# An earlier release for one weights load, and one conversion a step earlier, in a fused attention and feed-forward kernel

## The chip, the cores and the metric

The kernel runs on one core of a Trainium2 chip. The metric is the device time of one execution in microseconds (us). The kernel before takes 544.36 us (median of 3 runs, 543.9 to 545.09).

The core's engines work side by side, each in the order in which its instructions stand. TensorE (PE in the profile, its weight loads PEld) multiplies matrices, VectorE (DVE) and ScalarE (ACT) work elementwise, GpSimd (POOL) makes masks and constants here, and SyncE (SP) issues most of the transfers (DMAs). Engines wait for each other through semaphores.

## The reference, cut to what matters

A linear attention (4 batches, 8 heads, 768 positions, head size 48) feeds a feed-forward block (3072 tokens, width 384, inner width 2048).

```python
for t in range(S):
    cur = einsum('bhd,bhe->bhde', u[None] * kt, vt)
    y[:, :, t] = einsum('bhd,bhde->bhe', rt, state + cur)
    state = wt[:, :, :, None] * state + einsum('bhd,bhe->bhde', kt, vt)

x = y.transpose(0, 2, 1, 3).reshape(B * S, H * D)
h = x @ w_in
out = (h - tanh(h)) @ w_out
```

## The kernel before

**Tiling.** The 3072 tokens are eight blocks of 384 (four batches, two halves of the sequence each). Attention goes by chunks of 64 tokens. For a block it is made of scores inside a chunk ("own", the diagonal, and "earlier", the part off the diagonal), updates (each chunk's keys times values, from which the states follow) and results (scores times values plus states times receptances). The eight heads lie in four pairs, and the pairs in two halves, `HALVES`: `h1` is handled first, then `h2`.

**Feed-forward.** A block's feed-forward has 16 steps `f`. A step multiplies the block's `x` with one tile of `w_in` (three matmuls of 128x384; the profile counts two for each, so six, L871), copies the product out on ScalarE (`h`, L876), forms the activation on VectorE and ScalarE (the square L902, ScalarE's square `qa` L905, two products L879), and a few steps later multiplies with a tile of `w_out` (L950 in block 0). While one block's feed-forward runs, the next block's attention is made in its steps, by a written plan: `plan(i)` says which piece belongs to which step.

**Weights.** The weights arrive as 64-bit raw words in 16 units of 768 KB (`load_weights`, L251). A unit alternates between `w_in` and `w_out`, in the order of `UNITS`, and holds the tiles of two steps. `convert` turns a unit into float32 pairs with three operations on ScalarE (L264: one into `w_sb`, two into a scratch tile `up`) and then one merge on VectorE (L268, in place in `w_sb`). A matmul with a tile of that unit waits for the merge. Five raw buffers rotate.

**Boot.** Before block 0's feed-forward can start, `boot` makes block 0's attention with nothing to hide it behind. Its order is written out by hand: every engine's instructions stand in the order of the calls. PE's order in the first part is: small matmuls that only keep PE busy (L312, L305), own scores of h1 (L494), a transposition (L517), earlier scores of h1 (L494 again), updates of h1 (L616), a transposition, then results of h1 (L697, L679), then the same for h2.

SP issues in the boot: the inputs of block 0, raw unit 0, raw unit 1 (the "second raw weights"), then some small pieces of `xT` and further units. `begin_behind(ins, then)` adds a wait: `then` does not begin before `ins` is done. For raw unit 1 the instruction waited for is `blk.done`, the last matmul of whatever `gram` or `update_half` last set it.

**Conversions in block 0.** From unit 2 on, conversions are spread over block 0's steps. `PIECES[f]` says how many of ScalarE's conversion operations step `f` takes. In `converting` they come from one list, three per unit; the merge goes with the third. All but one of a step's operations stand ahead of `qa`, the last behind it. The merges of a step (`made_up`) are run by VectorE in the next step (`extra`), ahead of that step's square. A step's loads (`loads` in `plan`) wait for the step's copy of its product on ScalarE.

The unit whose merge step 8 needs is the eighth, `(0, 4)`: its third operation stands in step 6 before the change.

Of the kernel before, what the change touches and what calls it, by code (L numbers as in the profile page):

```python
# [72 lines left out]
RAWS = 5  # L73
LAG = 2
LAST = 5
PIECES = 0, 0, 2, 3, 3, 2, 4, 4, 3, 3, 3, 4, 4
UNITS = [(0, 0), (0, 1)] + [u for j in range(NF // 2 - 2) for u in ((1, j), (0, j + 2))] + [(1, NF // 2 - 2),
                                                                                      (1, NF // 2 - 1)]
LATE = 3
# [47 lines left out]
def kernel(  # L127
# [12 lines left out]
    nc = tc.nc  # L140
# [107 lines left out]
    def load_weights(n, queue):  # L248
        raw = conv.tile([P, 2 * DM, 2], I32, name="raw", tag="raw")
        src = weights[UNITS[n]].bitcast(I32).rearrange("p (n two) -> p n two", two=2)  # L250
        return *UNITS[n], raw, queue.dma_start(out=raw, in_=src)  # L251

    def convert(part, j, raw, _, tiles=1):

        lo, hi = raw[:, :, 0], raw[:, :, 1]
        a = w_sb[:, part, 2 * j:2 * j + 2].rearrange("p f c -> p (f c)").bitcast(I32)
        up = conv.tile([P, 2 * DM], I32, name="up", tag="up", bufs=4)
        low, high = (up.bitcast(t).rearrange("p (n two) -> p n two", two=2)[:, :, i]  # L260
                     for i, t in enumerate((U16, F16)))

        def scaled(to, of, scale, bias=0.0):
            return lambda: nc.scalar.activation(out=to, in_=of, func=AF.Copy, scale=scale, bias=bias)  # L264

        return [scaled(a.bitcast(F32), hi.bitcast(F32), HIGH_SCALE), scaled(high, hi.bitcast(F32), SIGN_SCALE),
                scaled(low, lo.bitcast(U32), *LOW)], [
                lambda of=slice(i * 2 * DM // tiles, (i + 1) * 2 * DM // tiles): nc.vector.scalar_tensor_tensor(  # L268
                    out=a[:, of], in0=a[:, of], scalar=3, in1=up[:, of], op0=ALU.logical_shift_left,
                    op1=ALU.bitwise_or) for i in range(tiles)]  # L270
# [43 lines left out]
    def begin_behind(ins, then):  # L314
        tc.add_manual_dep(then.ins, ins.ins.name, mybir.DependencyInfo(
            mybir.DependencyClass.Sync, mybir.DependencyReason.DATA))
# [3 lines left out]
    class Block:  # L320
# [186 lines left out]
        def own(self, ps, p0, **fill):  # L507
            return self.masked(ps, "k", "r", masks["diagonal"], p0, **fill)

        def earlier(self, ps, p0, **fill):  # L510
            return self.masked(ps, "post", "pre", masks["above"], p0, **fill)
# [370 lines left out]
    def slight(h, n, i, f):  # L882

        s, qa = (dense.tile([P, NB], F32, name=name, tag=name) for name in ("s", "qa"))
        q, j = divmod(f, 2)
        if i in fast:
            g = G[:, g_at(q, "0" + "ab"[j]):g_at(q, "2" + "ab"[j]) + 1].rearrange("p t c -> p (t c)")
        else:  # L890
            g = ring(sums, 0, n)
        if n in light:
            at = 2 * blocks_n + light.index(n)
            nc.scalar.activation(out=s, in_=h, func=AF.Square)  # L894
            nc.scalar.activation(out=qa, in_=s, func=AF.Square, bias=shift[:, 4:5])  # L895
            junk = work.tile([P, UP * NCH * LP], BF16, name="junk", tag="junk", bufs=1)
            nc.scalar.activation(out=junk[:, 0:NB], in_=s, func=AF.Relu, bias=shift[:, 5:6],  # L897
                                 accum_out=excess[:, at:at + 1])
            square = first = []
        else:  # L900
            at = plain.index(n)
            square = [lambda: nc.vector.tensor_tensor_reduce(  # L902
                out=s, in0=h, in1=h, scale=1.0, scalar=0.0, op0=ALU.mult, op1=ALU.max,
                accum_out=top[:, at:at + 1])]
            first = [lambda: nc.scalar.activation(out=qa, in_=s, func=AF.Square, bias=shift[:, 4:5])]  # L905
        return g, first, square, [product(h, h, TOP, s, ALU.mult), product(g, qa, REST, h, ALU.add)]
# [198 lines left out]
    def more_weights(queue):  # L1105
        raws.append(load_weights(more_weights.n, queue))
        more_weights.n += 1
        return raws[-1][-1]
# [3 lines left out]
    def run(ops):  # L1112
        for op in ops:
            op()

    def converting(pieces, n):

        made = []
        for _ in range(n):
            if not pieces:  # L1120
                on_act, on_dve = convert(*raws.pop(0))
                pieces += zip(on_act, ([], [], on_dve))
            op, then = pieces.pop(0)
            op()
            made += then
        return made

    def boot(ps, pair, blk, later):
        h1, h2 = HALVES
        blk.tiles["w"] = states0  # L1130
        for name, p0, n in (("w", h1 + 1, 1), ("w", h1, 1), ("k", h1, UP), ("r", h1, UP), ("w", h2, UP)):
            blk.load(name, p0, n)
        blk.load_v()
        blk.load("k", h2, UP)
        blk.load("r", h2, UP)
        more_weights(nc.sync)

        both = (h1, h1 + 1), (h2, h2 + 1)
        blk.behind(h1 + 1, 1)
        blk.behind(h1, 1)  # L1140
        blk.take_whole(h1, UP)
        blk.totals_by_column(h1)
        nc.scalar.copy(out=later_ident, in_=ident)
        blk.before(h1, UP)
        blk.times_behind(h1, UP)
        blk.times_u(h1, UP)
        own = blk.own(ps, h1, spare=94, ahead=5, late=6)
        blk.turn_1(ps, h1)
        blk.times_before(h1, UP)
        earlier = blk.earlier(ps, h1)  # L1150
        blk.behind(h2, UP)
        blk.take_whole(h2, UP)
        first_a, first_b = convert(*raws.pop(0), tiles=2)
        own()
        blk.turn_2(h1)
        blk.totals_by_column(h2)
        blk.update_half(pair, h1)
        begin_behind(blk.done, more_weights(nc.sync))
        blk.times_behind(h2, UP)
        blk.times_u(h2, UP)  # L1160
        blk.turn_1(ps, h2)
        blk.turn_2(h2)
        earlier()
        blk.results(ps)
        blk.result("from_scores", both[0])
        run(blk.states_half(h1))
        blk.result("from_states", both[0], True, apart=True)
        blk.before(h2, UP)
        blk.update_half(pair, h2)
        blk.times_before(h2, UP)  # L1170
        own = blk.own(ps, h2)
        own_scored = blk.done
        run(first_a[:1])
        blk.result_out((3,), [nc.scalar.copy] * 2)
        blk.result_out((2,))
        earlier = blk.earlier(ps, h2, ahead=1)
        scored = blk.done
        onwards = blk.states_half(h2)
        own()
        run(first_a[1:])  # L1180
        needed = 2 * KC - 2
        blk.fill_holes([nc.sync, nc.gpsimd], range(needed, 2 * KC))
        begin_behind(own_scored, more_weights(nc.sync))
        blk.fill_holes([nc.sync, nc.gpsimd], range(needed))
        begin_behind(scored, more_weights(nc.sync))
        later.load("w")
        second_a, second_b = convert(*raws.pop(0))
        third_a, third_b = convert(*raws.pop(0))
        run(second_a)
        more_weights(nc.sync)  # L1190
        blk.results(ps)
        blk.yp.reverse()
        blk.result("from_states", both[1], apart=True)
        earlier(1, 1)
        earlier(0, 1)
        for p in reversed(both[1]):
            blk.result("from_scores", (p,), True, more=True)
        later.load("k")
        more_weights(nc.sync)
        run(onwards)  # L1200
        run(first_b[:1])
        for p in reversed(both[1]):
            blk.result_out((p,), [nc.scalar.copy, nc.vector.tensor_copy])
        run(first_b[1:])
        run(third_a[:2])
        run(second_b)
        blk.held(0, NPAIR)
        return [(third_a[2], third_b)]
# [6 lines left out]
    with tc.tile_pool(name="ps_boot", bufs=1, space=PSUM) as ps_boot:  # L1215
        pieces = boot(Turns([scratch(ps_boot)] + ps_a.both), [hp] + acc, blocks[0], blocks[1])
# [30 lines left out]
    for i, blk in enumerate(blocks):  # L1247
# [9 lines left out]
        for f in range(NF):  # L1257
# [6 lines left out]
            if not i:  # L1264
                made_up = converting(pieces, (PIECES[f] if f < len(PIECES) else 1) - 1)
                for op in ahead_of_h:
                    op()
                made_up += converting(pieces, 1 if f < len(PIECES) and PIECES[f] else 0)
            g, ahead_of_h, square, later_ops = slight(h, now, i, f)
# [184 lines left out]
```

## Time and profile before

| | |
|---|---|
| median of 3 runs | 544.36 us (543.9 to 545.09) |
| the profiled execution | 545.84 us, of which its span is 544.1 |
| PE busy | 533.7 us, 98% of the span |
| DVE busy | 459.0 us, 84% |
| ACT busy | 403.8 us, 74% |
| mean granted TensorE clock | 0.995 |
| chain that ended last | PE 95%, DVE 2%, issue 1% |

Times in the profile count from the span's start. A row of the timeline or of the chain of waits has start, duration, engine, line and operation; "x6" is a count, and the brackets behind a timeline row say how long the engine stood idle before it and what ended that. "issue" is time in which an engine waited for nothing that the profile shows. A row of a windows table has the window, its length, then busy time and count of instructions for PE, PEld, DVE, ACT and POOL, the granted TensorE clock, the busy share of the DMA engines and GB/s. A row of the DMA queues has packets, MB and the packets' time as a share of 16 engines times the window.

Block 0's feed-forward begins at 25 us, so the boot is the first 25 us; the other seven blocks are PE's work almost without a gap.

### The profile page before, as it was taken

The page shows a single profiled execution, that of the slowest core. Times are in us where ns is not written, and L with a number is a line of the kernel's source. Part 1 is how long each engine was busy: PE and PEld are TensorE (multiplying, and loading weights), DVE is VectorE, ACT ScalarE, POOL GpSimd, SP SyncE. Part 2 cuts the span into 40 slices and gives each one's busy share as a digit, 9 for nine tenths or more (in the row PEclk, how much of TensorE's full clock was granted, in tenths as well). Part 3 has the DMA queues.
Part 4 walks back from the last instruction along what each step waited for, and adds up shares of the span by engine and source line. Part 5 has one row for each costly group of instructions (what it writes and reads, how often), then busy time and mean ns, then how long its engine had stood idle before and what let it go on. Part 6 is the DMA issues. An engine that isn't in the chain of part 4 may idle for free.

```text
span 544.1 us, 14866 instructions
## 1 busy us (share of the span) xinstructions
PE 533.7 (98%) x5682; PEld 404.1 (74%) x5682; DVE 459.0 (84%) x943; ACT 403.8 (74%) x814; POOL 6.6 (1%) x47
## 2 busy tenths in 40 slices
PE   7899999999999999999999999999999999999996
PEld 5756666678887788777877787877878787787874
DVE  7889999999989989789897979879897997457564
ACT  5799996888668876688676886588866885666561
POOL 1100000000000000000000000000000000000000
PEclk9899999999999999999999999999999999999999
DMA  7798633251402631154212532137231420200101
GB/s 274 236 400 308 237 102 115 87 146 60 121 19 79 159 110 54 58 128 138 60 55 73 121 116 67 49 89 161 67 97 54 92 56 2 57 1 0 45 1 46
DMA packets 53048, 56.34 MB, mean 104 GB/s; under 512 B 21488, under 2 KB 50928, under 8 KB 52976
## 3 DMA queue, kind: packets, MB, share of 16 engines
q1 hardware_dynamic: 52592, 55.18, 33.8%
q8 instruction: 48, 0.79, 0.6%
q14 instruction: 24, 0.20, 0.1%
q10 hardware_dynamic: 288, 0.10, 0.1%
q0 software_dynamic: 96, 0.07, 0.1%
HBM read 44.73 MB, written 4.72 MB: 91 GB/s over the span
## 4 chain that ended last, share of the span: by engine, by line
PE 95%; DVE 2%; issue 1%; DMA 0%; PEld 0%; PEldq 0%; DVEq 0%; SPq 0%
PE hp L871 44%; PE acc L999 26%; PE att L999 7%; PE acc L950 5%; PE att L757 4%; PE att L494 2%; PE acc L977 2%; PE att L575 1%; PE att L871 1%; PE acc L871 1%; DVE post L429 1%; DVE scores L502 1%; DMA states<-in_wT 0%; DVE pre L417 0%; PE att L977 0%
## 5 line engine op out<-in xcount | busy, mean ns | idle before, releaser
L871 PE MATMUL hp<-xT,w_sb 128*128 128x384 f32 x738 | 259.2, 487 | 0.4 <-DVE w_sb L268 0.4
L871 PEld LDWEIGHTS hp<-xT,w_sb 128*128 128x128 f32 x738 | 131.9, 190 | 69.7 <-issue 0.5
L999 PE MATMUL acc<-forms,g 128*128 128x128 f32 x954 | 133.2, 276 | 0.0
L876 ACT ACTIVATE h<-hp 128x384 f32<-128x384 f32 x123 | 60.4, 491 | 97.3 <-PE hp L871 97.1
L999 PEld LDWEIGHTS acc<-forms,g 128*128 128x128 f32 x954 | 122.0, 192 | 10.3
L879 DVE SCALAR_TENSOR_TENSOR h<-h,s 128x384 f32<-128x384 f32 x128 | 70.5, 551 | 50.5 <-ACT s L894 50.4
L920 DVE TENSOR_TENSOR g<-g 128x256 f32<-128x256 f32 x265 | 103.1, 418 | 7.3 <-PE acc L999 6.5
L895 ACT ACTIVATE qa<-s,shift 128x384 f32<-128x384 f32 x113 | 69.5, 615 | 3.7
L897 ACT ACTIVATE junk<-s,shift 128x384 bf16<-128x384 f32 x113 | 67.7, 599 | 0.0
L879 DVE SCALAR_TENSOR_TENSOR g<-qa,h 128x384 f32<-128x384 f32 x112 | 61.6, 550 | 1.6 <-ACT qa L905 0.2
L894 ACT ACTIVATE s<-h 128x384 f32<-128x384 f32 x113 | 59.1, 523 | 3.5
L999 PEld LDWEIGHTS acc<-w_sb,g 128*128 128x128 f32 x318 | 46.8, 191 | 9.7 <-ACT sums L967 0.3
L999 PE MATMUL acc<-w_sb,g 128*128 128x128 f32 x318 | 53.1, 276 | 0.0
L999 PE MATMUL att<-w_sb,g 128*128 128x128 f32 x212 | 35.5, 275 | 0.0
L999 PEld LDWEIGHTS att<-w_sb,g 128*128 128x128 f32 x212 | 31.1, 192 | 5.3
L1034 DVE TENSOR_TENSOR sums<-sums 128x256 f32<-128x256 f32 x84 | 32.8, 406 | 1.7 <-ACT sums L1011 1.5
L950 PE MATMUL acc<-w_sb,sums 128*128 128x384 f32 x96 | 33.7, 487 | 0.0
L264 ACT ACTIVATE up<-raw 128x768 f16<-128x768 f32 (+1 forms) x32 | 33.1, 1069 | 0.0
L950 PEld LDWEIGHTS acc<-w_sb,sums 128*128 128x128 f32 x96 | 18.0, 190 | 12.3 <-DVE sums L879 0.3
L417 DVE TENSOR_TENSOR_SCAN pre<-w,start 128x780 f32<-128x780 f32 x14 | 25.0, 1783 | 0.8
L429 DVE TENSOR_TENSOR_SCAN post<-w,seed 128x780 f32<-128x780 f32 x14 | 24.8, 1774 | 0.0
L897 ACT ACTIVATION_READ_ACCUMULATOR junk<-s,shift 128x1 f32 x113 | 21.1, 187 | 0.0
(118 smaller groups left out, 529.2 us busy)
## 6 DMA issues: line engine op xcount, KB each, us to landing
raw<-in_weights SPq DMA_DIRECT2D x16, 768.0 KB, 5.9
w<-in_wT SPq DMA_DIRECT2D x7, 780.0 KB, 4.6
k<-in_kT SPq DMA_DIRECT2D x7, 768.0 KB, 4.6
r<-in_rT SPq DMA_DIRECT2D x7, 768.0 KB, 4.6
v_sb<-in_v SPq DMA_DIRECT2D x8, 576.0 KB, 3.9
k<-in_tokens SPq DMA_DIRECT2D x7, 576.0 KB, 5.2
r<-in_tokens SPq DMA_DIRECT2D x7, 576.0 KB, 4.7
out_y<-sums SPq DMA_DIRECT2D x18, 128.0 KB, 1.8
```

The source lines that it names most:

```text
L264: return lambda: nc.scalar.activation(out=to, in_=of, func=AF.Copy, scale=scale, bias=bias)
L429: return nc.vector.tensor_tensor_scan(out=back(t[:, 0:width]), data0=back(self.tile("w")[:, a:a + width]), data1=back(seed[:, 0:width]), i ...
L871: nc.tensor.matmul(hp, lhsT=w_in_sb[:, f, kc, :], rhs=xT[kc], start=(kc == KC - 1), stop=(kc == 0))
L876: return h, nc.scalar.activation(out=h, in_=hp, func=AF.Copy, scale=1.0 / UPSCALE)
L879: return lambda: nc.vector.scalar_tensor_tensor(out=out, in0=in0, scalar=scalar, in1=in1, op0=op0, op1=ALU.mult)
L894: nc.scalar.activation(out=s, in_=h, func=AF.Square)
L895: nc.scalar.activation(out=qa, in_=s, func=AF.Square, bias=shift[:, 4:5])
L897: nc.scalar.activation(out=junk[:, 0:NB], in_=s, func=AF.Relu, bias=shift[:, 5:6], accum_out=excess[:, at:at + 1])
L920: return lambda: nc.vector.tensor_tensor(out=G[:, to:to + 2], in0=two(G, g_at(q, a0), g_at(q, a1)), in1=two(G, g_at(q, b0), g_at(q, b1)), ...
L950: nc.tensor.matmul(acc, lhsT=g[:, j * P:(j + 1) * P], rhs=w_out_sb[:, f, :], start=(f == self.first), stop=(f == NF - 1))
L999: nc.tensor.matmul(to, lhsT=G[:, g_at(q, a), :], rhs=rhs, start=start, stop=stop, skip_group_check=True)
L1034: ops.append(lambda op=op, at=at: nc.vector.tensor_tensor(out=at[0], in0=at[1], in1=at[2], op=OPS[op]))
```

## The change

Two things change.

1. In `boot`, the issue of raw unit 1 on SP is moved up in the text, so that `blk.done` is the last matmul of h1's earlier scores instead of the last matmul of h1's updates. SP's own order stays the same, since nothing else is issued on SP between the two places.
2. `PIECES[5]` goes from 2 to 3 and `PIECES[6]` from 4 to 3. One conversion operation, the third of unit `(0, 4)`, is done in step 5 instead of step 6, and the merge that hangs on it is run by VectorE in step 6 instead of step 7.

```diff
-PIECES = 0, 0, 2, 3, 3, 2, 4, 4, 3, 3, 3, 4, 4
+PIECES = 0, 0, 2, 3, 3, 3, 3, 4, 3, 3, 3, 4, 4
...
         blk.times_before(h1, UP)
         earlier = blk.earlier(ps, h1)
+        begin_behind(blk.done, more_weights(nc.sync))
         blk.behind(h2, UP)
         blk.take_whole(h2, UP)
         first_a, first_b = convert(*raws.pop(0), tiles=2)
...
         blk.turn_2(h1)
         blk.totals_by_column(h2)
         blk.update_half(pair, h1)
-        begin_behind(blk.done, more_weights(nc.sync))
         blk.times_behind(h2, UP)
         blk.times_u(h2, UP)
         blk.turn_1(ps, h2)
```

## The prediction

> **What bounds the kernel now.** I read the page's head first, then the chain of waits over the first 60 us, then who waited for whom on TensorE, then short windows around the two places that the diff touches.
>
> ```profile
> span 544.1 us, 14866 instructions
> PE 533.7 (98%) x5682; PEld 404.1 (74%) x5682; DVE 459.0 (84%) x943; ACT 403.8 (74%) x814; POOL 6.6 (1%) x47
> ```
>
> PE is busy for 533.7 of 544.1 us, so all that can be won or lost in place is some 10 us of PE idle time, nearly all of it in the boot, plus whatever the boot does to the clock. PE's two waits after the first 17 us that are long enough to matter are these:
>
> ```profile
> PE att L494 <- issue: 1.2, 1, 1.2
> PE hp L871 <- DVE w_sb L268: 0.4, 1, 0.4
> ```
>
> The chain of waits places them:
>
> ```profile
> 19.14 0.61 PE att L494 x29
> 19.75 1.22 issue
> 20.97 0.50 PE att L494 x18
> ...
> 53.19 0.95 DVE w_sb L268
> 54.13 0.14 issue
> 54.27 2.17 PE hp L871 x6
> ```
>
> The first stall cuts the second half's off-diagonal scores in two, after 29 of 48 matmuls, and no engine is named as its cause. The second is step 8's first product waiting for DVE to finish a weight tile. Each part of the change aims near one of them.
>
> For the first I looked at what PE executes per stretch (times, then PE and PEld with their counts), and at the packets of the queue marked "instruction" (16 KB each; one row per window of 0.1 us, so the last column times 1.6 us is the packet's duration):
>
> ```profile
> 12.40:16.74 4.34, 3.94 (x139) 3.42 (x132) 4.27 (x9) 3.03 (x6) 0.00 (x0) 1.00 0.63 216
> 16.74:20.90 4.16, 2.89 (x134) 2.34 (x132) 4.13 (x5) 4.11 (x7) 1.58 (x3) 1.00 0.36 82
> ```
>
> ```profile
> q8 instruction: 1, 0.02, 58.1%
> ...
> q8 instruction: 1, 0.02, 83.0%
> ...
> q8 instruction: 1, 0.02, 64.7%
> ...
> q8 instruction: 1, 0.02, 64.1%
> ```
>
> The four packets begin at 7.67, 13.96, 18.54 and 23.22 (the windows from 7.6, 13.9, 18.5 and 23.2) and take 0.93, 1.33, 1.04 and 1.03 us. The two stretches hold some 270 PE instructions each, a dozen of which were already running at their start. So PE uses up about 256 in each, which is 16 KB at 64 bytes, one packet. Counted back from the stall at 19.75, blocks end at 16.75, 12.40 and 4.54. The block that PE lacks at 19.75 is the packet of 18.54: it lands at 19.57, and PE goes on at 20.97, 1.39 later. With the same 1.39, the packet of 13.96 is usable at 15.28 + 1.39 = 16.67, and PE reaches that block's first instruction at 16.75. The next packet begins 1.79 after that. So from 12.4 to 21 the boot runs at the pace of instruction packets, about 4.2 us per block: a delay of the packet of 13.96 comes out at 20.97 undiminished, and a gain too.
>
> The Trainium skill (Runtime: NRT & Kernel Launch, Instruction fetch mechanics) says that an engine's instructions are refilled in 16 KiB blocks of 256 and that crossing a block is mostly hidden. The trace agrees on the block, and differs on the hiding: 1.22 us are exposed here. By the page's rule alone the first term of the sum below would be 0 instead of +0.15.
>
> The stall costs a second time:
>
> ```profile
> 16.60:20.01 3.41, 3.03 (x138) 2.48 (x134) 3.38 (x4) 3.36 (x6) 1.58 (x3) 1.00 0.28 87
> 20.01:23.42 3.41, 2.28 (x67) 2.14 (x67) 2.85 (x7) 2.53 (x3) 0.13 (x2) 1.00 0.87 269
> 23.42:26.83 3.41, 3.34 (x51) 2.52 (x52) 1.76 (x4) 2.20 (x4) 0.00 (x0) 0.50 0.96 350
> ```
>
> After a stretch with PE busy for 2.28 of 3.41 us (67%) the granted clock is 0.50 for the next 3.41 us. With 3.03 busy (89%) it stayed at 1.00. The half clock is worth up to 3.41 x 0.5 = 1.7 us.
>
> **Part 1: the second raw weights' load is released earlier.** PE's, SP's and POOL's instruction orders are unchanged: this is a wait moved on SP. Rows of the timeline:
>
> ```profile
> 4.53 2.14 PE L305 MATMUL att<-ident 128*128 128x512 bf16 x5
> ...
> 5.65 8.21 SPq L251 DMA_DIRECT2D raw<-in_weights  x2
> ...
> 11.23 0.93 PE L494 MATMUL att<-pre,post 48*64 48x64 f32 x48
> ```
>
> Its time from issue to landing, and ScalarE's first read of its buffer:
>
> ```profile
> raw<-in_weights SPq DMA_DIRECT2D x1, 768.0 KB, 4.5
> ```
>
> ```profile
> 19.80 0.86 ACT L264 ACTIVATE w_sb<-raw 128x768 f32<-128x768 f32 x1
> ```
>
> The second issue ends at 5.65 + 8.21 = 13.86; one issue is about 0.33, so it starts at 13.53. The scores that release it in the changed kernel end at 11.23 + 0.93 = 12.16; with the same 0.1 us to SP it starts at about 12.27, 1.26 earlier. Nothing queues behind it on SP before 18.04, so no other issue moves. Its landing goes from 13.53 + 4.5 = 18.0 to about 16.8. Nobody waits for that: ScalarE's first read of this buffer is at 19.80, right behind other conversions, so 1.8 us of margin become 3.1. The direct gain is 0.
>
> What it can touch is the packet of 13.96. Today the load of 13.53 moves its bytes from about 14.5 on; moved up by 1.26, its stream is already running from about 13.2 when that packet is to begin. Two terms. *Start:* the packet of 23.2 began inside such a stream, 2.26 us after PE got into the block before (20.97 to 23.22), against 1.79 with the queues empty (16.75 to 18.54): +0.47. The low end is 0, since the packet of 13.96 began 1.56 after 12.40 beside the first load's tail. The high end is the first packet, 7.67, which began 3.1 after its block's 4.54 under the full opening loads: 3.1 - 1.56 = +1.6. I take +0.45, as one weights load in flight is what the 23.2 row has. *Duration:* today's 1.33 has the second load's beginning in its middle; the other two take 1.03 to 1.04, one of them (23.2) inside a running stream. I take -0.30; ends -0.30 and 0. Sum of part 1: **+0.15 us**, ends -0.30 and +1.6.
>
> **Part 2: one conversion on ScalarE goes from step 6 to step 5, and its VectorE merge from step 7 to step 6.** The order of the two programs shows just this: one "up" conversion stands ahead of the square of step 5 instead of behind the copy of step 6's product, and one of the two merges at 53.19 stands between the two scans. Nothing is added or removed. ScalarE's, VectorE's and the weight load's rows:
>
> ```profile
> 46.07 0.49 ACT L876 ACTIVATE h<-hp 128x384 f32<-128x384 f32 x1
> ```
>
> ```profile
> 47.91 1.78 DVE L417 TENSOR_TENSOR_SCAN pre<-w,start 128x780 f32<-128x780 f32 x1
> ...
> 53.19 1.80 DVE L268 SCALAR_TENSOR_TENSOR w_sb<-w_sb,up 128x768 int32<-128x768 int32 x2
> ...
> 76.66 0.54 DVE L879 SCALAR_TENSOR_TENSOR sums<-qa,h 128x384 f32<-128x384 f32 x1
> ```
>
> ```profile
> 77.25 1.61 PEld L950 LDWEIGHTS acc<-w_sb,sums 128*128 128x128 f32 x6 [0.32 <-DVE sums L879]
> ```
>
> On ScalarE the copy of step 6's product slips by one conversion, 0.92, from 46.07 to about 47.0; its bank is written again by step 7's product, which now starts near 48.7, so 1.2 us of cover remain, and behind it ScalarE has the same work at the same times. The weights' load of step 6, which waits for that copy, slips by the same 0.92; its buffer is read some 18 us later. On VectorE the merge that step 8 needs runs at about 49.7 instead of 53.19 and is done near 50.6. The sums behind it slip by 0.87, to about 52.2, and PE reads them at 56.3: covered. So PE's 0.45 at 54 goes; step 8 starts when the updates' matmuls end.
>
> But VectorE does the same work in total, and from 29.6 to 77.2 it is in one unbroken row: 46.19 of 47.61 us busy.
>
> ```profile
> 29.59:77.20 47.61, 47.16 (x322) 28.77 (x320) 46.19 (x84) 46.73 (x67) 0.13 (x2) 1.00 0.76 275
> ```
>
> So its sums at 76.66 end at 77.20 in both kernels, and PE's weight load at 77.25 waits for exactly these. Today PE loses nothing by it, but has no margin either. A PE that is 0.45 early stands there for 0.45. The stall moves from 54 to 77. I take 0; ends -0.45 (if VectorE wins as much) and 0.
>
> **Sum.** +0.15 + 0 = +0.15 on the profiled execution's own 545.84 us (span 544.1 and 1.74 around it), which is 1.5 above the median of 544.36 of the runs shown. On that median: 544.5 us.
>
> **Rivals.**
> *Slower: the instruction packet queues behind the weights.* If the packet of 13.96 must wait as the first one did, PE runs dry at 16.75, and again at 19.75 plus as much: +1.6, so 546.0. For it: the packet at 7.67, in the one stretch where loads were stacked before it. Against it: the packet of 13.96 began while the first load's last pieces still ran. It decides from 1.1 us of delay on. The Trainium skill (DMA: Bandwidth & Descriptors, Queues, rings and completion order) has each DMA engine change between queues only after a whole packet, often of 9 to 17 descriptors, which speaks against this change; the row of 23.2, begun 0.47 late in full traffic, bears it out only in part.
> *Faster: the half clock goes.* If the packet of 13.96 just becomes 0.30 shorter, the stall at 19.75 ends 0.30 earlier and the stretch in front of the gate is fuller: 2.58 of 3.41 us, 76%. Where that is enough, the half clock's 1.7 go as well: -2.0, so 542.4. It decides somewhere between the 67% and the 89% seen. For it: the three clock rows. Against it: it needs the start not to slip. The Trainium skill (TensorE: Matmul & The Clock Gate, What you observe and its table) has the gate fall after an idle window of about 3.4 us; here 1.2 us idle in one window did it.
> *The gain at 54 is kept:* -0.45, 543.9, if VectorE's row is not what ends the weight load at 77.25.
>
> **How the numbers follow.** Forecast 0.40, gain kept 0.05, both inside 0.2% of 544.36 (1.1 us either way, 543.3 to 545.4, about what a measurement of this kernel can tell from no change): same 0.45. Packet queues: slower 0.35. Clock: faster 0.20. The forecast's own range is 544.36 - 0.75 to 544.36 + 0.47, 543.6 to 544.8. For 8 in 10 it reaches up over the slower rival, to 546.2, and down to 543.0, which leaves out most of the clock's case.
>
> **What would show it.** Right: the second weights' issue near 12.3; an instruction packet that begins at 14.0 to 14.5 and takes about 1.0; PE's issue stall still 1.2 us, ending at 20.8 to 21.5; no PE wait for a weight merge near 54, and one of about 0.4 us for VectorE's sums near 77. Wrong: a second issue stall near 16.8, or a packet that begins after 15 (slower); a granted clock of 1.00 through 23 to 27 (faster); no wait near 77 (the 0.45 kept). The prediction is most exposed in the packet's start, which the kernel before shows only under other loads.

## The result, and the profile after

The changed kernel takes 548.79 us (median of 6) against 544.31 of the kernel before: slower by a factor of 1.0076, 95% interval 1.005 to 1.0102. The forecast was no change, 544.5, in a range of 543.0 to 546.2. The profiled execution after is the fastest of its runs, 547.99 us, and that of before, 545.84, is slower than most of its; so the two traces show 2.2 us of the 4.4.

First the page's head, and who waited for whom on PE, of the changed kernel:

```profile
span 546.3 us, 14866 instructions
PE 537.4 (98%) x5682; PEld 406.4 (74%) x5682; DVE 459.4 (84%) x943; ACT 403.8 (74%) x814; POOL 6.5 (1%) x47
```

```profile
PE att L679 <- issue: 0.7, 1, 0.7
...
PE acc L950 <- DVE sums L879: 0.2, 1, 0.2
```

PE's waits have changed places. The stall without a named cause is now in h1's results (L679), one instruction block earlier than the one of before. The wait for a weight merge is gone, and one for VectorE's sums has come.

The second weights' load is issued 1.3 us earlier, as the diff says: its issue ends at 12.56 instead of 13.86. Here is SP's row, and then the two instruction packets that follow (windows from 15.8 and from 19.9, each of 0.1 us, so 61.1% is 0.98 us and 72.1% is 1.15 us):

```profile
5.24 7.32 SPq L251 DMA_DIRECT2D raw<-in_weights  x2
```

```profile
q8 instruction: 1, 0.02, 61.1%
...
q8 instruction: 1, 0.02, 72.1%
```

The packet that began at 13.96 now begins at 15.82. The records of the single pieces say why: the load's 6 KB pieces, eight per DMA engine, run from about 13.2 on. On all DMA engines but one the last piece ends between 15.77 and 15.93, and the instruction packet starts within 0.01 us of such an end. From 13.2 to 15.82 the queues carry this and no instruction packet (q1 is the queue of the loads):

```profile
q1 hardware_dynamic: 149, 0.82, 98.1%
```

The packet has landed at 16.80. PE used up its block at 17.1, and goes on at 18.06:

```profile
12.40:17.09 4.69, 4.10 (x141) 3.51 (x134) 4.49 (x9) 3.23 (x6) 0.00 (x0) 1.00 0.65 214
17.09:18.06 0.97, 0.25 (x6) 0.10 (x4) 0.97 (x1) 0.65 (x2) 0.49 (x1) 1.00 0.00 0
```

Then the granted clock falls, and stays down three times as long as before:

```profile
15.31:18.72 3.41, 2.40 (x72) 2.02 (x64) 3.31 (x6) 2.30 (x6) 1.10 (x2) 1.00 0.16 64
18.72:22.13 3.41, 3.31 (x99) 2.73 (x100) 2.64 (x4) 3.41 (x5) 0.48 (x1) 0.50 0.20 43
22.13:25.55 3.42, 3.42 (x84) 3.08 (x79) 1.85 (x6) 1.16 (x2) 0.13 (x2) 0.50 0.96 265
25.55:28.96 3.41, 3.17 (x53) 2.43 (x52) 1.57 (x3) 2.01 (x4) 0.00 (x0) 0.50 0.93 360
```

A stretch with PE busy for 2.40 of 3.41 us is followed by three at 0.50 (10.24 us in all, where the kernel before had 3.41), although PE is busy for nearly all of them. The chain of waits gives what it comes to when block 0's third product begins, and what is left when block 1's results begin. Before, then after:

```profile
30.01 1.94 PE hp L871 x6
...
79.48 1.49 PE att L757 x95
```

```profile
32.23 1.94 PE hp L871 x6
...
81.69 1.49 PE att L757 x96
```

The boot loses 2.22 us, and the 49.5 us behind it take 49.47 before and 49.46 after. All of the difference between the traces is in the first 32 us, and part 2 has changed nothing.

### The profile page after: what moved, and what is told of

The parts are those of the page before. It is cut to its first block, busy times and chain, and to the rows that moved or that the text cites. A ratio compares the mean times of both kernels' runs of the same rounds, so it can differ in the third digit from the quotient of the medians.

```text
span 546.3 us, 14866 instructions
## 1 busy us (share of the span) xinstructions
PE 537.4 (98%) x5682; PEld 406.4 (74%) x5682; DVE 459.4 (84%) x943; ACT 403.8 (74%) x814; POOL 6.5 (1%) x47
## 4 chain that ended last, share of the span: by engine, by line
PE 93%; DVE 2%; DMA 2%; issue 1%; PEld 1%; SPq 1%; PEldq 0%; DVEq 0%
PE hp L871 43%; PE acc L999 26%; PE att L999 6%; PE acc L950 5%; PE att L757 4%; PE att L494 2%; PE acc L977 2%; DMA k<-in_kT 2%; PE att L575 2%; PE att L871 1%; PE acc L871 1%; DVE first_states L631 1%; SPq L369 0%; DVE pre L417 0%; PE att L977 0%
```

## The experiments

Each run names its median and its ratio to the kernel before on the same chip, with the 95% interval. Theory A: instruction packets stand behind the weights' pieces that were queued before them. Theory B: the loss comes from part 2. Theory C: only the place of the load's release matters, not its size. Theory H: a good part of the loss is the half clock that follows a dry spell (a stretch in which PE has no instructions).

### Each part alone

Part 1 alone:

```diff
 PIECES = 0, 0, 2, 3, 3, 2, 4, 4, 3, 3, 3, 4, 4      (as before)
+        begin_behind(blk.done, more_weights(nc.sync))   # behind earlier(h1)
...
-        begin_behind(blk.done, more_weights(nc.sync))   # behind update_half(h1)
```

> The kernel before with part 1 alone: the second raw weights' load waits for h1's earlier scores. Theory A (the instruction packet of 13.96 stands behind this load's pieces on its DMA engine): the whole loss is here, about 548.5 us; the packet begins near 15.8 instead of 13.96, PE runs dry near 17 to 18, and block 0's first product starts near 27.3 instead of 25.0. It also keeps PE's 0.45 us wait for a weight merge, near 56.5. Theory B (the loss comes from the conversion moved on ScalarE): no change, 544.3.

548.73 us, 1.0059 (1.0037 to 1.0081). The packet begins at 16.06. PE is without instructions twice, and PE's wait for a weight merge, 0.5 us here, is still there. The waits on PE:

```profile
PE att L494 <- issue: 1.5, 1, 1.5
...
PE att L679 <- issue: 0.7, 1, 0.7
...
PE hp L871 <- DVE w_sb L268: 0.5, 1, 0.5
```

Part 2 alone:

```diff
-PIECES = 0, 0, 2, 3, 3, 2, 4, 4, 3, 3, 3, 4, 4
+PIECES = 0, 0, 2, 3, 3, 3, 3, 4, 3, 3, 3, 4, 4
```

> The kernel before with part 2 alone: one conversion in step 5 instead of 6. Theory A: 544.1 to 544.4, no change that can be measured; the 0.45 us wait for a weight merge near 54 is gone and a wait of 0.3 to 0.45 us for VectorE's sums stands near 77, so that the results of block 1 start within 0.1 us of where they did, 79.4. If the gain is kept, 543.9 and the results start near 79.0. Theory B: 548.5.

544.09 us, 0.9986 (0.9969 to 1.0003): nothing that can be measured. The wait for the merge is gone, and the chain runs through VectorE's sums near 75 instead:

```profile
74.78 0.47 DVE sums L879
75.25 0.04 issue
75.30 2.20 PE acc L950 x6
77.50 1.49 PE att L757 x96
```

The weight load of that row waits 0.83 us for the sums, instead of 0.32 before:

```profile
75.30 1.59 PEld L950 LDWEIGHTS acc<-w_sb,sums 128*128 128x128 f32 x6 [0.83 <-DVE sums L879]
```

By PE's rows, block 0's third product begins at 27.86 and block 1's results at 77.43, 49.57 us later; in the kernel before it is 29.84 and 79.41, also 49.57. So what PE wins in step 8 is handed back. Theory B is out, and the loss is part 1's. All rows here stand some 2 us earlier than before, although the boot is the same: in this execution PE's dry spell in h2's scores is 0.46 instead of 1.22 us, and the clock stays at 1.00.

### Where the load is released

A quarter early, the rest in the old place:

```diff
+        begin_behind(blk.done, more_weights(nc.sync, 32))       # partitions 0 to 31, behind earlier(h1)
...
+        begin_behind(blk.done, rest_of_weights(nc.sync, 32))    # the others, behind update_half(h1)
```

> The kernel before, with a quarter of the second raw weights (32 of 128 partitions, so two pieces per DMA engine instead of eight) released by h1's earlier scores, and the other three quarters where the whole load was. Theory A (the packet waits for as many pieces as are queued ahead of it on its engine): two pieces are through before 14.5, so the packet begins at 14.0 to 14.6 and the time is 544.3 to 545.0. Theory C (any weights stream that starts there holds the packet, whatever its size): the packet begins near 15.8 and the time is near 548.

545.81 us, 1.0028 (1.001 to 1.0045): more than expected. The profiled execution is its fastest, 544.49, and in it the packet begins at 13.29, ahead of everything; so its trace doesn't show where the other executions lose. Four of the ten, with a mean granted clock of 0.992 to 0.994, take 546.5 to 548.2, and the others 544.5 to 545.9.

Half early, the same edit with 64 partitions:

> The kernel before, with half of the second raw weights (64 partitions, four pieces per DMA engine) released by h1's earlier scores and the other half where the whole load was. Theory A (the instruction packet waits for the pieces queued ahead of it): the early half is through near 14.7 to 15.0, and if the late half, issued at 13.5, lines up behind it before the packet does, near 15.8 as with the whole load; so 545.5 to 548.8, at or above the quarter's 545.8. Theory C (any stream that starts there): the same as the quarter, 545.8, whatever the size.

548.98 us, 1.0058 (1.0032 to 1.0085), as much as the whole load, and just above the range of theory A. In the profiled execution (548.54) the packet begins at 15.29 (window from 15.2; 72.9% is 1.17 us):

```profile
q8 instruction: 1, 0.02, 72.9%
```

That is within 0.01 us of the end of a fourth piece, the last of the early half on its DMA engine, and the pieces of the second half, issued at 13.44, run from 15.2 on. So the packet stood behind the early half alone, and began 0.5 us earlier than in the changed kernel. That saved no time: the granted clock was 0.50 for 10.24 us here too. Two of ten executions are at 544.8, with a mean granted clock of 0.999 and 1.0, and the other eight at 548.4 to 549.9, with 0.988 to 0.992, and nothing between. That fits a packet that comes either ahead of the early half or behind it; of the two no trace was taken. The quarter lost less than the half, which speaks against theory C, but the intervals of the two ratios overlap.

Later than before, behind the transposition for h2:

```diff
         blk.turn_1(ps, h2)
+        begin_behind(blk.turned_by, more_weights(nc.sync))   # the last transposition
```

> The kernel before with the load moved the other way: it waits for the transposition of h2's keys, some 0.8 us later than before, so it is issued near 14.3. Theory A: the packet of 13.96 has no new weights beside it and takes 1.0 instead of 1.33 us, so PE's 1.22 us stall becomes about 0.9, if the stream is through before the next packet at 18.2; 543.5 to 544.3. If the stream reaches into that next packet, it begins late and the time is 544.5 to 546. ScalarE's first read of the buffer at 19.80 does not wait in either case, or by under 0.3.

544.92 us, 1.0014 (0.9997 to 1.003). The packet has no new weights beside it and takes 1.18 instead of 1.33 us, and the next one is not late (18.27), but the hoped-for gain did not come: the time lies where theory A put a late next packet.

Later still, behind h1's results from scores:

```diff
         blk.result("from_scores", both[0])
+        begin_behind(blk.done, more_weights(nc.sync))
```

> The kernel before with the second raw weights' load released still later, by the last of h1's results from scores (near 15.1), so that its stream runs from about 16.2 to 19. Theory A: now it is the next instruction packet, that of 17.4 to 18.5, that stands behind the stream: it begins near 18.8 to 19.3, PE's dry spell at 19.75 lasts until 21.2 to 21.7, and the time is 544.8 to 546.5. ScalarE's first read of this buffer, at 19.80, waits by under 0.5 us, which would cost little, as PE does not need that unit before its second step. Theory C (the place near 13 alone is sensitive): 544.3, no change.

547.39 us, 1.0051 (1.0032 to 1.007). The packet of 13.8 is on time, and it is the next one that is late: it begins at 19.67 instead of 18.54, and PE's dry spell in h2's scores grows from 1.22 to 1.65 us. The chain of waits goes by the weight loads (PEld), which stand still for 1.78 us:

```profile
19.65 0.54 PEld att L494 x29
20.19 1.78 issue
21.97 0.42 PEld att L494 x18
```

This is what theory A says, and theory C, by which the time would be 544.3, is out: whichever packet is asked for while the stream is queued is the one that waits. The loss was larger than expected, as here too the half clock came for 6.83 instead of 3.41 us. Over the traces the packet begins one stream after the load's issue: 12.21 to 15.82 in the changed kernel, 12.17 to 16.06 with part 1 alone, 15.77 to 19.67 here, which is 3.6 to 3.9 us each time.

### The packet asked for earlier

The changed kernel with 32 PE instructions more at its start, so that block boundaries come earlier in the work:

```diff
-        own = blk.own(ps, h1, spare=94, ahead=5, late=6)
+        own = blk.own(ps, h1, spare=110, ahead=5, late=6)
```

> The changed kernel with 110 instead of 94 tiny matmuls at the start: 32 PE instructions more, so that every boundary between instruction blocks comes 32 instructions earlier in the work, and the packet that was late is asked for near 11.6, before the second weights' load is issued at 12.2. Theory A (order of asking): the packet begins near 13.3 to 14.0, right behind the first load, PE no longer runs dry near 17, and the time comes down to 544 to 545.5. If pieces that are queued later still go first, the packet begins near 15.8 and the time stays at 548 to 549.

546.75 us, 1.0039 (1.0025 to 1.0053). The load is where the changed kernel has it, issued at 12.20, and the packet begins at 13.2, and PE's first dry spell is gone. So it is the order of asking that decides. The time does not come down to the 545.5 expected because a later boundary has moved too: the packet for h2's results begins at 22.4, behind the third weights' stream, and PE waits there. The packets in the windows from 13.2 and 22.3, and PE's wait:

```profile
q8 instruction: 1, 0.02, 68.6%
...
q8 instruction: 1, 0.02, 68.8%
```

```profile
PE att L697 <- issue: 1.2, 1, 1.2
```

### The clock

The kernel before with more of the matmuls on constants that only keep PE busy, in front of its dry spell:

```diff
-        earlier = blk.earlier(ps, h2, ahead=1)
+        earlier = blk.earlier(ps, h2, ahead=5)
```

> The kernel before with five instead of one of the matmuls that only keep PE busy ahead of h2's earlier scores (eight PE instructions and about 0.85 us of PE work more), in front of the place where PE runs dry at 19.75. Theory H (part of the loss is the half clock after the dry spell): the stretch before the gate is fuller, the granted clock is 1.00 through 23 to 27 in every execution, and the times lie closer together, 543.8 to 544.6, without the runs at 545.5 to 547.5; block 0's first product does not start later than 24. Rival: the extra matmuls only push PE's work back, 544.9 to 545.5.

544.24 us, 0.9991 (0.9979 to 1.0002). The ten executions lie between 543.95 and 545.09, where 27 of the kernel before beside them went from 543.89 to 547.0, and all ten have a mean granted clock of 0.998 or more. Ten executions are few for this, though: part 2 alone, without the fill, has none above 544.9 either. Block 0's first product begins at 24.14 in the trace, just after the 24 expected. The clock is 1.00 throughout in the trace (from 20 to 30 us):

```profile
20.00:30.00 10.00, 9.76 (x165) 6.58 (x163) 8.12 (x17) 8.98 (x14) 0.13 (x2) 1.00 0.97 341
```

The mean granted clock of each execution is known, and it goes with the time. Of the 98 executions of the kernel before beside all these runs, 17 have 0.995 or less and take 545.99 to 547.59 us. Of the other 81 all but three take 543.59 to 545.41.

The same fill in the changed kernel, ahead of the two places where its packets come late:

```diff
         blk.results(ps)
+        busy(blk.yp[0][:, 0], 4)
         blk.result("from_scores", both[0])
...
-        earlier = blk.earlier(ps, h2, ahead=1)
+        earlier = blk.earlier(ps, h2, ahead=5)
```

> The changed kernel with PE kept busy in front of both dry spells: four more matmuls on constants ahead of h1's results, and five instead of one ahead of h2's earlier scores (16 PE instructions and 1.7 us of PE work more). The instruction packet stays as late as in the changed kernel (begins near 15.8). Theory H (some 2 us of the changed kernel's 4.4 are the half clock that follows the dry spells): the granted clock is 1.00 from 9 to 30, and the time is 546.0 to 547.0. Rival (the late packets alone make the 4.4 us): 548.5 to 550.

547.57 us, 1.0043 (1.0023 to 1.0064): about 1 us under the changed kernel, not 2. The clock stays at 1.00 in the trace (in seven of the ten executions the mean is 0.998 or more; their median is 547.26) and the packet is as late as ever (15.90):

```profile
9.00:20.00 11.00, 9.44 (x339) 7.86 (x342) 10.07 (x14) 6.81 (x12) 1.23 (x3) 1.00 0.57 213
20.00:30.00 10.00, 8.23 (x178) 5.68 (x171) 6.42 (x14) 7.20 (x11) 0.48 (x3) 1.00 0.81 276
```

Here PE has a third wait, of 0.7 us, before block 0's first products; the profile puts it down to VectorE's copy into `xT`, but an instruction packet, landed at 26.45, would become usable at the same moment if it took the 1.39 us of the kernel before. To take the added instructions out again:

```diff
-        own = blk.own(ps, h1, spare=94, ahead=5, late=6)
+        own = blk.own(ps, h1, spare=86, ahead=5, late=6)
```

> The changed kernel with the same fill as in the run before it, and 86 instead of 94 tiny matmuls at the start, so that the 16 added instructions are taken out again ahead of the fill and the block boundaries behind it stand where they stood in the changed kernel. Theory H: the third dry spell, near 26.6, which the fill had brought by moving a boundary in front of block 0's first products, is gone, the granted clock is 1.00, and the time is 546.0 to 546.8: the late packets alone are then about 2 us of the loss, the half clock the rest. Rival: 547.5 or more, and the half clock is not the rest.

548.25 us, 1.0045 (1.0024 to 1.0066). This missed its aim: with 16 instructions fewer at the start, the first block boundary is reached at 7.7 instead of 4.5, its packet begins at 11.65 instead of about 8, and PE runs dry in h1's updates instead:

```profile
PE acc L616 <- issue: 1.3, 1, 1.3
```

So this run says nothing on the clock's share, and one thing more on the packets.

Fill and part 2 together, with the load where it was:

```diff
-PIECES = 0, 0, 2, 3, 3, 2, 4, 4, 3, 3, 3, 4, 4
+PIECES = 0, 0, 2, 3, 3, 3, 3, 4, 3, 3, 3, 4, 4
...
-        earlier = blk.earlier(ps, h2, ahead=1)
+        earlier = blk.earlier(ps, h2, ahead=5)
```

> The kernel before with part 2 of the change and the five matmuls ahead of h2's earlier scores (as in the run with the fill), and the load where it was. If both do what they did alone: 543.9 to 544.4, with no execution above 545.2; against the kernel before's median of 544.5 a gain of 0.05 to 0.1%, at the edge of what can be measured. Rival: the two do not add up, since the one only moves a wait and the other only takes away the half clock in some executions: 544.2, as with the fill alone.

544.39 us, 0.9996 (0.9984 to 1.0008). The two do not add up to a gain; no execution is above 545.15, against 547.49 beside it.

### The changed kernel once more

> The changed kernel itself beside the run with the fill on the same chip: 548 to 549.5, with its first packet of the dry spells beginning at 15.5 to 16.1 and a granted clock of 0.50 somewhere between 18 and 31.

548.37 us, 1.0044 (1.0013 to 1.0076). Seven of ten executions are at 547.9 to 549.6, and three at 543.9 to 544.0, as fast as the kernel before at its best. The profiled one is of the seven (packet at 15.97, half clock for 10.24 us). In the changed kernel the load is issued at 12.2, and PE gets into the next instruction block at 12.3 to 12.4: a tie, which would explain that the packet comes first now and then. The three have a mean granted clock of 0.998 to 1.0 and the seven 0.987 to 0.993, which fits. No trace of the three was taken, so this is argued and not shown.

## Why the prediction was wrong

**What bounds the boot** was right: from 12.4 to 21 us it goes at the pace of instruction packets, and a late packet comes out at the end. It does not come out undiminished: with the packet 1.86 late, PE goes on in h2's scores 1.62 later than in the trace of before, and 2.30 later than in that of part 2 alone.

**Part 1, direct effects** were right: nobody waits for this buffer, and SP's next issue comes only at 18.81.

**Part 1, the packet's start** is the step that failed. It was sized at +0.45 with a high end of +1.6, and measured +1.86 (13.96 to 15.82). What the prediction had named as a sign of being wrong, a packet that begins after 15, is what came. The fault is the row chosen. The packet of 23.22 was taken as "begun inside such a stream", 0.47 late, and read as a small fee. But its wait was the rest of a stream that was nearly over: the issue of that load went from 18.87 to 19.92, and the packet began 3.30 after its end. In the changed kernel, with part 1 alone and behind the scores it is 3.27 to 3.56 from the end of the issue. A wait that lasts until something else ends has no price of its own; it must be worked out from where in the stream the question falls. For a packet asked for just as the stream is queued, that is all of it: it begins 3.6 to 3.9 us after the load's issue starts.

**Part 1, the packet's duration** was right in sign (0.98 instead of 1.33 us) and too small to matter.

**The slower rival** named the mechanism, the place and the first dry spell, and was given 0.35; it should have been the forecast. Its price of 1.6 was too low, for two reasons. The delay of the packets alone came to 2.3 us: in the run with part 2 alone, whose clock stayed at 1.00, PE goes on in h2's scores at 20.29, and in the changed kernel at 22.59. And the rival left out the half clock, which the prediction counted only as something that could go away. From there to block 0's third product the changed kernel lost another 1.9 us against that run (32.06 - 27.86 - 2.3), at half clock. The sum, 4.2, is near the 4.4 between the medians; 0.2 of it is won back later, as the spans of the two traces differ by 3.98.

The changed kernel with the fill bears both shares out. PE's rows, first of part 2 alone and then of that run:

```profile
20.29 0.50 PE L494 MATMUL att<-pre,post 48*64 48x64 f32 x18 [0.46 <-issue]
...
27.86 2.10 PE L871 MATMUL hp<-xT,w_sb 128*128 128x384 f32 x6
```

```profile
22.75 0.62 PE L494 MATMUL att<-pre,post 48*64 48x64 f32 x26 [0.79 <-issue]
...
27.85 3.46 PE L871 MATMUL acc<-xT,w_sb 128*128 128x384 f32 x10 [0.73 <-DVE xT L729]
31.15 2.10 PE L871 MATMUL hp<-xT,w_sb 128*128 128x384 f32 x6
```

With the clock held at 1.00, PE still goes on only at 22.75, so that delay is the packets'. From there to the third product it takes 8.40 us, of which 0.73 is the new wait; without it 7.67, near the 7.57 of part 2 alone, where the changed kernel takes 9.47 at half clock. The new wait is why the time came down by about 1 us and not by 1.9. These are single traces; how the 4.4 us between the medians divide is an estimate from them.

**The rule of whole packets** (the Trainium skill, DMA: Bandwidth & Descriptors, Queues, rings and completion order) spoke against this change, and was right about the direction. The traces agree with it: the instruction packet began only after all eight pieces of the stream on its engine in the changed kernel, and after the four of the early half, ahead of the second, in the run with a half. The Trainium skill's rule that instruction block boundaries are mostly hidden (Runtime: NRT & Kernel Launch, Instruction fetch mechanics) does not hold in this boot, where PE stands for 1.22 us at one boundary before and for 0.72 at another after.

**Part 2** was right: PE's 0.45 at 54 went, it came back as a longer wait for VectorE's sums (at 75.3 in part 2 alone, at 79.5 in the changed kernel), and no worth of it can be measured.

**The sum's base** hid something: the profiled execution of before had the half clock, which most of its executions don't have (81 of 98 are above 0.995 in the mean), and a dry spell of 1.22 us, where the same boot in the trace of part 2 alone has 0.46. So the rows of one trace were not the usual state, and the loss from the clock could only grow.

**The reading of the clock** by PE's busy share alone, 67% against 89%, was too simple. In the same trace a stretch with 59% was followed by a clock of 1.00:

```profile
6.36:9.77 3.41, 2.02 (x32) 0.87 (x30) 3.41 (x4) 1.17 (x3) 0.00 (x0) 1.00 1.05 371
9.77:13.18 3.41, 3.27 (x138) 2.71 (x133) 3.38 (x5) 1.38 (x3) 0.00 (x0) 1.00 0.95 365
```

## What to carry to other kernels

In a stretch with many short instructions, the instruction stream is itself a transfer with due times: find the block boundaries in the trace, see when each packet is asked for, and keep large loads from being queued just ahead of it. Moving a load that nobody waits for is not free; ask what is queued behind it on the DMA engines, instructions included. And where a step is made cheaper on one engine, look for the next place where another engine's unbroken row ends: a gain that is handed back there is worth nothing.

## What the runs showed of the hardware that was not expected

- An instruction packet of 16 KB began 3.6 to 3.9 us after the issue of a 768 KB load queued ahead of it, in three kernels with two release places, and at 13.2, about 1 us after the load's issue, where it was asked for first.
- The granted clock fell to 0.50 after stretches of 3.41 us with PE busy for 67% and 70%, and in the changed kernel stayed there for 10.24 us although PE was busy all but 0.1 us of the first two of the three stretches. In those two nearly all of PE's work is on tiles of 48 to 64 rows and columns. The stretches after which the clock came back (23.42 to 26.83 before, 25.55 to 28.96 after) end in products of 128x128 tiles, from 24.95 and from 27.27 on. The stretch of 59% that kept the clock has mostly matmuls of 128x512. That the size of the tiles counts beside the busy share is a reading of these stretches, and no run tests it.
- In the changed kernel, 32 PE instructions more at the start of the program moved PE's dry spell from h1's results to those of h2 (1.2 us), and 16 fewer, with the fill behind them, moved it to h1's updates (1.3 us).
